# First eight attention units of a fused attention and two-layer network: mask added on TensorE, one exponential per unit, row sums from a column of ones, first loads in program order, weight scaling on ScalarE

## The chip, the cores and the metric

The kernel runs on one core of one Trainium2 chip. The metric is device time in microseconds (us) of one execution; runs of a kernel are given by their median. Engines are called as in the profile: PE is TensorE (PEld its weight loads), DVE is VectorE, ACT is ScalarE, SP is the engine whose queue issues the DMAs here. Every engine runs its own list of instructions strictly in the order of that list, and waits where an operand isn't there yet.

## The reference

Three parts follow each other. The first is attention with 4 batches, 8 heads, 512 local and 32 global positions, 64 numbers a head. A local position sees the global keys and the local keys at most 32 positions away:

```python
s_ll = np.where(np.abs(pos[:, None] - pos[None, :]) <= 32, s_ll, -1e9)
a_l = softmax(np.concatenate([s_lg, s_ll], axis=-1))      # sum + 1e-9 below the line
out_l = np.matmul(a_l, np.concatenate([v_g, v_l], axis=2))
```

Global positions see everything. The result, 2176 rows of 512, goes through `x @ w_in`, a leaky ReLU with a slope of its own for each of the 2048 hidden columns, and `@ w_out`; then through a second layer pair with hard-swish. Weights come to the chip as 64-bit floats seen as integers, so the kernel makes 32-bit floats of them, and each of these is split into a high and a low part for TensorE, so that a product takes three passes (high times high, low times high, high times low).

## The kernel before

**Attention.** A unit is one batch, one half of its 512 rows and one pair of heads: 32 units, taken two at a time. `load` (L166) fetches queries and keys of a unit into `qk_t` (four buffers), `load_v` (L172) its values. `scores` (L182) does the unit's 16 products of 32 rows by 128 keys for two banks of PSUM (one per head). `softmax` (L199) then runs four DVE instructions a unit that add the mask, take the minimum of the negated scores and leave both (L212), four ACT exponentials of 128 columns that also sum their row (L216), and two small DVE instructions that add 1e-9 and invert the sum (L218, L220). `transposes` (L222) does four PE transposes and one ACT copy (L229), `values` (L231) 16 products with the values and one DVE multiplication by the inverted sum (L246), which gives `xo`.

**First layer, block 0.** The tokens of units 0 to 7 (batch 0) are block 0, in two lanes of 256 tokens: lane 0 is units 0 to 3, lane 1 units 4 to 7, four steps (`DELAY`) later. `x_from_attention` (L400) transposes `xo` on PE, and ACT and DVE split it into high and low (L395, L396: `xt`). At each step `h_tile` does 12 products a lane for one hidden chunk (L424), `act` the leaky ReLU on ACT and DVE (L434, L436) and the split of the result (L442, L443: `g`), and `y_tiles` 12 products a lane with the second weights (L455). After block 0 come four more blocks with weights that are on the chip by then, then the second layer pair.

**Weights of the first layer.** There are 32 halves, called raw 0 to raw 31 here, in the order in which they are needed: chunk 0 in, chunk 1 in, chunk 0 out, chunk 2 in, chunk 1 out, chunk 3 in, and so on. Each is a 512 KB DMA into one of five buffers (L94). `to_float32` (L103) makes 32-bit floats of it: a ReLU on ACT over the low words (L109), a scaling of the high words by a power of two on DVE (L113), and two DVE instructions that put the parts together (L117, L119). `split_w` (L123) then casts on ACT to the high part (L125) and subtracts on DVE for the low part (L126). So a half costs ACT two instructions and DVE four:

```python
here(nc.scalar.activation(low, low, AF.Relu, bias=quarter_sb, scale=0.9 * 2.0 ** -29))
if on_dve:
    here(nc.vector.tensor_scalar(out=z, in0=high.bitcast(F32), scalar1=2.0 ** -112, ...))
else:
    here(nc.scalar.activation(z, high.bitcast(F32), AF.Copy, scale=2.0 ** -112))
```

**What sets the order.** The order of each engine's list is made when the kernel is built, by a scheduler with its own estimate of times; `here` (`keep_in_program_order`) ties an instruction to its place in the program. The DMAs of units and weights all go through SP's list, which the scheduler orders too. Buffers of PSUM turn over: what is written next into a bank waits for whoever reads it.

Of the kernel before, what the change touches and what calls it, by code (L numbers as in the profile page):

```python
# [10 lines left out]
F32 = mybir.dt.float32  # L11
# [15 lines left out]
NEG = -1.0e30  # L27
# [15 lines left out]
CONVERT = (3, 4, 5)  # L43
# [12 lines left out]
def fused_kernel(ctx, tc, qkE, vE, qgz, kN, vN, vgN, w1, w2, consts, out):  # L56
# [9 lines left out]

    consts_sb = const.tile([128, 4 * 128 + NJ], F32, name="consts_sb")
# [53 lines left out]
    def split_w(raw, wt, m):  # L123
        z = to_float32(raw)
        nc.scalar.copy(wt[:, m, 0, :], z)  # L125
        nc.vector.tensor_tensor(out=wt[:, m, 1, :], in0=z, in1=wt[:, m, 0, :].bitcast(F32), op=ALU.subtract)  # L126

    class Weights:
# [13 lines left out]
        def fetch(self, upto):  # L142
            while self.got < min(upto, 2 * NJ):
                self.raw[self.got] = load_raw(self.src, *self.seq[self.got])
                self.got += 1

        def convert(self, halves):
            for _ in range(halves):
# [7 lines left out]
                split_w(self.raw.pop(k), self.wt[j], m)  # L156
# [6 lines left out]
    def local_units(att):  # L163
        units = [(b, hf, hp) for b in range(B) for hf in range(2) for hp in range(HP)]
        q_t, k_t, v_t, p_t, rs_t, pt_t, v2 = {}, {}, {}, {}, {}, {}, {}
        def load(u):  # L166
            b, hf, hp = units[u]
            qk = att.tile([128, 256 + UNIT_K], F32, tag="qk", name="qk_t", bufs=PRE + 1)
            nc.sync.dma_start(out=qk, in_=qkE[b, hf, hp])
            q_t[u], k_t[u] = qk[:, 0:256], qk[:, 256:256 + UNIT_K]  # L170

        def load_v(u):  # L172
            b, hf, hp = units[u]
            if u < FIRST_UNITS:
# [24 lines left out]
        def softmax(u, s):  # L199
            b, hf, hp = units[u]  # L200
            if u < FIRST_UNITS:
                if u == 0:
# [4 lines left out]
            st = att.tile([128, 4, 4], F32, tag="st", name="st", bufs=4)
            for i in range(2):
                m = 1 if (hf, i) == (0, 0) else 2 if (hf, i) == (1, 1) else 0
# [9 lines left out]
            rs_t[u] = att.tile([128, 4], F32, tag="rs", name="rs", bufs=FIRST_UNITS)  # L219
# [11 lines left out]
        def values(*us):  # L231
            o = bank("o_ps")
# [44 lines left out]
        load_v(4)  # L277
        load_v(5)
# [663 lines left out]
    W1.fetch(2)  # L942
    k = 0
# [65 lines left out]
def _layout(q_l, k_l, v_l, q_g, k_g, v_g, moe_w_in, moe_w_out, moe_alpha, moe2_w_in, moe2_w_out):  # L1009
# [17 lines left out]
    vE = con(vw.reshape(B, HP, 2, 16, 128, D).transpose(0, 1, 4, 3, 2, 5))  # L1027
# [9 lines left out]
    def chunks(w_in, w_out):  # L1037
# [31 lines left out]
```

## Time and profile before

| | us |
|---|---|
| median of 3 runs | 840.61 (839.18 to 841.01) |
| the profiled execution | 838.92 |
| its span, first to last instruction | 836.8 |
| PE busy in the span | 817.8 (98%) |
| DVE busy | 594.1 (71%) |
| ACT busy | 415.4 (50%) |

The profiled execution is 1.7 us below the median. Outside its span lie 2.1 us. PE is busy nearly always, so the places where it isn't are what there is to look for; "busy" counts pipelined matmuls from start to modelled end, so a slowed row of matmuls can look busy too. A view by stretches gives the busy time of each engine in each; where an engine is busy all the time in a stretch in which PE waits, that engine is the bound there. A group's "idle before" is the time that its engine stood still just ahead of it.

### The profile page before, as it was taken

The numbers are of one execution on the slowest core, as the hardware profiler recorded it, in microseconds if no ns is written. First come the engines' busy times: TensorE is split into PE (matmuls) and PEld (weight loads), VectorE is DVE, ScalarE is ACT, GpSimd is POOL, SyncE is SP. The second block draws the span as 40 slices with busy tenths as digits, with TensorE's granted clock in tenths as the row PEclk, the third lists the DMA queues.
The fourth block names the chain that finished last, engine by engine and source line by source line (L and its number), as shares of the span: only waits on it lengthen the run. The fifth ranks groups of instructions, "written<-read, shape, count | busy, mean of one in ns | idle before, by whom it ended". The sixth has DMA issues, their size and how long they took to land.

```text
span 836.8 us, 18274 instructions
## 1 busy us (share of the span) xinstructions
PE 817.8 (98%) x7228; PEld 740.3 (88%) x7228; DVE 594.1 (71%) x1319; ACT 415.4 (50%) x905; POOL 0.2 (0%) x4
## 2 busy tenths in 40 slices
PE   6889999999999999989999999999999999999997
PEld 4779999888888888878899988889999999999996
DVE  4999995477878786787678847778867678854221
ACT  5876665455656554455454523434543444432222
POOL 0000000000000000000000000000000000000000
PEclk9999999999999999999999999999999999999999
DMA  9976563367768876798575555666675878788872
GB/s 334 340 267 239 181 215 119 109 210 254 272 215 296 270 253 238 256 312 297 182 263 203 166 200 190 193 208 215 201 239 199 295 255 284 243 280 262 276 255 67
DMA packets 72868, 195.70 MB, mean 234 GB/s; under 512 B 7120, under 2 KB 18384, under 8 KB 72784
## 3 DMA queue, kind: packets, MB, share of 16 engines
q1 hardware_dynamic: 72688, 194.42, 68.8%
q8 instruction: 57, 0.93, 0.4%
q14 instruction: 27, 0.22, 0.1%
q10 hardware_dynamic: 96, 0.13, 0.1%
HBM read 152.05 MB, written 42.47 MB: 232 GB/s over the span
## 4 chain that ended last, share of the span: by engine, by line
PE 86%; DVE 6%; DMA 3%; ACT 3%; issue 1%; SPq 0%; DVEq 0%; ACTq 0%
PE y_ps L455 20%; PE h_ps L424 19%; PE o_ps L859 17%; PE k_ps L776 16%; PE h_ps L928 4%; PE o_ps L714 4%; DMA raw<-in_w 2%; PE o_ps L240 1%; PE s_ps L194 1%; DVE z L117 1%; PE pt_ps L227 1%; DVE z L119 1%; DVE wt L126 1%; DVE z L113 1%; PE xt_ps L409 1%
## 5 line engine op out<-in xcount | busy, mean ns | idle before, releaser
L455 PE MATMUL y_ps<-g,wt 128*128 128x256 f32 (+2 forms) x1152 | 209.3, 331 | 3.4 <-ACT g L442 1.7
L424 PE MATMUL h_ps<-xt,wt 128*128 128x256 f32 (+2 forms) x1152 | 206.3, 329 | 1.4 <-DVE xt L396 0.9
L455 PEld LDWEIGHTS y_ps<-g,wt 128*128 128x128 f32 x1152 | 176.5, 189 | 23.0 <-ACT g L442 2.1
L424 PEld LDWEIGHTS h_ps<-xt,wt 128*128 128x128 f32 x1152 | 177.8, 190 | 18.7 <-DVE xt L396 1.1
L859 PE MATMUL o_ps<-ws,gh 128*128 128x256 f32 x784 | 139.4, 283 | 0.0
L776 PE MATMUL k_ps<-bt,ws 128*128 128x512 f32 (+1 forms) x672 | 135.1, 362 | 0.0
L776 PEld LDWEIGHTS k_ps<-bt,ws 128*128 128x128 f32 x672 | 121.2, 188 | 13.0
L859 PEld LDWEIGHTS o_ps<-ws,gh 128*128 128x128 f32 x784 | 120.8, 192 | 0.1
L859 PE MATMUL o_ps<-ws,gl 128*128 128x256 f32 x392 | 107.0, 283 | 0.0
L790 DVE TENSOR_TENSOR gl<-far,gh 128x1024 fp32r<-128x1024 f32 (+1 forms) x56 | 60.9, 1089 | 33.0 <-ACT gh L789 32.7
L789 ACT CAST gh<-far 128x1024 fp32r<-128x1024 f32 (+1 forms) x56 | 52.7, 942 | 62.8 <-PE o_ps L859 58.5
L436 DVE SCALAR_TENSOR_TENSOR t<-t,c_sb,h_ps 128x256 f32<-128x256 f32 (+2 forms) x96 | 55.2, 588 | 32.3 <-ACT t L434 32.0
L859 PEld LDWEIGHTS o_ps<-ws,gl 128*128 128x128 f32 x392 | 73.5, 192 | 0.0
L434 ACT ACTIVATE t<-h_ps 128x512 f32<-128x512 f32 (+2 forms) x84 | 42.8, 511 | 52.9 <-PE h_ps L424 51.2
L442 ACT CAST g<-t 128x512 fp32r<-128x512 f32 (+2 forms) x84 | 45.3, 539 | 43.8 <-DVE t L436 43.7
L443 DVE TENSOR_TENSOR g<-t,g 128x512 fp32r<-128x512 f32 (+2 forms) x84 | 49.2, 587 | 21.3 <-ACT g L442 18.7
L761 ACT ACTIVATE t<-far,half_sb 128x512 f32<-128x512 f32 (+1 forms) x48 | 32.1, 671 | 50.9 <-DVE far L757 49.7
L216 ACT ACTIVATE p<-p,st 128x128 f32<-128x128 f32 x128 | 49.7, 390 | 11.9 <-DVE st L212 11.9
L109 ACT ACTIVATE raw<-raw,quarter_sb 128x512 uint32<-128x512 uint32 x64 | 49.6, 775 | 3.7 <-DMA raw<-in_w 3.7
L117 DVE SCALAR_TENSOR_TENSOR z<-z,raw 128x512 uint32<-128x512 uint32 x64 | 43.7, 691 | 3.3 <-ACT raw L109 0.8
L119 DVE SCALAR_TENSOR_TENSOR z<-raw,z 128x512 uint32<-128x512 uint32 x64 | 43.6, 689 | 0.7
L928 PE MATMUL h_ps<-xt,ws 128*128 128x384 f32 x192 | 36.0, 336 | 0.0
(100 smaller groups left out, 854.8 us busy)
## 6 DMA issues: line engine op xcount, KB each, us to landing
ws<-wo SPq DMA_DIRECT2D x72, 512.0 KB, 4.2
raw<-in_w SPq DMA_DIRECT2D x64, 512.0 KB, 5.4
ws<-wi SPq DMA_DIRECT2D x64, 512.0 KB, 4.6
v_t<-in_vE SPq DMA_DIRECT2D x32, 512.0 KB, 7.1
qk_t<-in_qkE SPq DMA_DIRECT2D x32, 368.0 KB, 5.5
wi<-raw SPq DMA_DIRECT2D x16, 512.0 KB, 3.1
wi<-parts SPq DMA_DIRECT2D x16, 512.0 KB, 4.5
wo<-raw SPq DMA_DIRECT2D x16, 512.0 KB, 4.0
```

Source lines behind the costliest of these rows:

```text
L109: here(nc.scalar.activation(low, low, AF.Relu, bias=quarter_sb, scale=0.9 * 2.0 ** -29))
L117: nc.vector.scalar_tensor_tensor(out=bits, in0=bits, scalar=3, in1=low, op0=ALU.logical_shift_left, op1=ALU.bitwise_or)
L119: nc.vector.scalar_tensor_tensor(out=bits, in0=high, scalar=0x80000000, in1=bits, op0=ALU.bitwise_and, op1=ALU.bitwise_or)
L216: nc.scalar.activation(p[:, n, :], p[:, n, :], AF.Exp, bias=st[:, 1, n:n + 1], scale=-1.0, accum_out=st[:, 2, n:n + 1])
L424: nc.tensor.matmul(ps[:, a:b], lhsT=wts[j][:, 0, wl, 128 * c:128 * c + 128], rhs=xt[c][:, xl, a:b], start=k == 0, stop=k == 3 * NC - 1)
L436: nc.vector.scalar_tensor_tensor(out=t[:, c:d], in0=t[:, c:d], scalar=c1_sb[:, j:j + 1], in1=ps[:, c:d], op0=ALU.mult, op1=ALU.add)
L455: nc.tensor.matmul(y[c][:, a:b], lhsT=wts[j][:, 1, wl, 128 * c:128 * c + 128], rhs=g[:, gl, a:b], start=first, stop=last, skip_group_check ...
L776: nc.tensor.matmul(bank, lhsT=wt[:, wl, at:at + 128], rhs=bt[x][:, c, xl, 0:w], start=first and k == 0, stop=k == 5, skip_group_check=True)
L789: nc.scalar.copy(hi, src)
L790: nc.vector.tensor_tensor(out=lo, in0=src, in1=hi.bitcast(F32), op=ALU.subtract)
L859: mm = nc.tensor.matmul(bank, lhsT=part[:, jp, 128 * c:128 * c + 128], rhs=wo[:, jp, 256 * wl:256 * wl + 256], start=opens, stop=k == NP / ...
L928: nc.tensor.matmul(h, lhsT=wt[:, wl, 128 * c:128 * c + 128], rhs=xt[c][:, xl, 0:w], start=k == 0, stop=k == 3 * NC - 1)
```

## The change

For units 0 to 7 (`FIRST_UNITS` is 8 and was 4; before, those units only had other buffers) the mask is now put into PSUM by a matmul of the identity with the mask, ahead of the score products, which add to it; ACT copies the mask and identity once into a tile of the matmul's type. DVE takes the row maximum of a whole bank (`tensor_reduce`) and subtracts it; one ACT exponential of 512 columns follows for each unit, with no sum. The values of these units get a column of ones (65 columns instead of 64), so the product itself gives the row sum, and DVE adds 1e-9, inverts and multiplies after the product. Units 0 and 1 go through scores one by one. The first loads are tied to program order, with values of units 0 and 1 ahead of queries and keys of units 2 and 3. All 32 halves of first-layer weights (`SCALED_ON_ACT`) have their scaling on ACT.

```diff
-NEG = -1.0e30
+NEG = -2.0 ** 100
-FIRST_UNITS = HP
+FIRST_UNITS = 2 * HP
+ORDERED = 5 * HP // 2
-CONVERT = (3, 4, 5)
+SCALED_ON_ACT = 32
+CONVERT = (2,3,4)
+    mask_r = wp.tile([128, 4 * 128], F32R, tag="w", name="mask_r", bufs=NJ)
...
-    def split_w(raw, wt, m):
-        z = to_float32(raw)
+    def split_w(raw, wt, m, on_dve):
+        z = to_float32(raw, on_dve)
...
-                split_w(self.raw.pop(k), self.wt[j], m)
+                split_w(self.raw.pop(k), self.wt[j], m, k >= SCALED_ON_ACT)
...
+        def first_scores(*us):
+            n, hf = 2 * len(us), units[us[0]][1]
+            s = [bank("s0_ps")[:, 0:128 * n], bank("s1_ps")[:, 0:128 * n]]
+            for h in range(2):
+                mask = mask_r[:, 128 * hf:128 * hf + 256]
+                nc.tensor.matmul(s[h].rearrange("p (e k) -> p e k", k=256), lhsT=mask_r[:, 384:512],
+                                 rhs=mask[:, None, :].to_broadcast([128, len(us), 256]), start=True, stop=False,
+                                 skip_group_check=True)
...
+                            nc.tensor.matmul(s[h][W * g:W * g + W, to:to + 128], lhsT=q[rows, at:at + W],
+                                             rhs=k[rows, o:o + 128], start=False, stop=True, skip_group_check=True)
...
+            for h in range(2):
+                x = s[h].rearrange("p (n k) -> p n k", k=128)
+                nc.vector.tensor_reduce(out=st[:, h, :], in_=x, axis=AX.X, op=ALU.max)
+                nc.vector.tensor_tensor(out=p.rearrange("p e (i h) k -> p h (e i) k", h=2)[:, h], in0=x,
+                                        in1=st[:, h, :, None].to_broadcast([128, n, 128]), op=ALU.subtract)
+            for e, u in enumerate(us):
+                nc.scalar.activation(p[:, e], p[:, e], AF.Exp, scale=0.125)
...
+        def first_values(*us):
...
+                        nc.tensor.matmul(o[W * g:W * g + W, n, :], lhsT=pt[:, n, W * g:W * g + W],
+                                         rhs=v[:, 4 * (n // 2) + g, n % 2, :], start=True, stop=True)
+                nc.vector.tensor_scalar(out=rs[:, 0, :], in0=o[:, :, D], scalar1=1e-9, scalar2=None, op0=ALU.add)
+                nc.vector.reciprocal(out=rs[:, 1, :], in_=rs[:, 0, :])
+                nc.vector.tensor_tensor(out=x.rearrange("p i (h d) -> p (i h) d", h=2), in0=o[:, :, 0:D],
+                                        in1=rs[:, 1, :, None].to_broadcast([128, 4, D]), op=ALU.mult)
...
         load(0)
-        nc.sync.dma_start(out=consts_sb, in_=consts)
+        here(nc.sync.dma_start(out=consts_sb, in_=consts))
+        nc.scalar.copy(mask_r, consts_sb[:, 0:512])
         load(1)
+        load_v(0)
+        load_v(1)
         load(2)
         load(3)
-        load_v(0)
-        load_v(1)
```

The change moves instructions on every engine. The first place is the head of SP's list. `qk_t` is queries and keys of a unit, `v_t` its values, `raw` a half of the weights. Before:

```order
L169 DMA qk_t<-in_qkE 128x736
L255 DMA consts_sb<-in_consts 128x528
L169 DMA qk_t<-in_qkE 128x736 x3
L180 DMA v_t<-in_vE 128x1024 x2
L94 DMA raw<-in_w 128x512
L180 DMA v_t<-in_vE 128x1024 x2
L94 DMA raw<-in_w 128x512
```

And now:

```order
L172 DMA qk_t<-in_qkE 128x736
L309 DMA consts_sb<-in_consts 128x528
L172 DMA qk_t<-in_qkE 128x736
L179 DMA v_t<-in_vR 128x1040 x2
L172 DMA qk_t<-in_qkE 128x736 x2
L99 DMA raw<-in_w 128x512
L179 DMA v_t<-in_vR 128x1040 x2
L99 DMA raw<-in_w 128x512
```

Values of units 0 and 1 stand ahead of queries and keys of units 2 and 3; raw 0 and raw 1 keep their places.

The second place is ACT's list around the softmax of units 4 and 5, with raw 3 to raw 6. L216 and L211 are exponentials, L109 and L111 the ReLU of a raw half, L118 its scaling, L125 and L127 the cast, L434 and L494 the leaky ReLU, L442 and L502 the split of its result, L229 and L281 the copy of transposed probabilities. Before:

```order
L109 ACTIVATE raw<-raw,quarter_sb 128x512
L125 CAST wt<-z 128x512 x2
L216 ACTIVATE p,st<-p,st 128x128 x3
L434 ACTIVATE t<-h_ps 128x256
L216 ACTIVATE p,st<-p,st 128x128 x5
L109 ACTIVATE raw<-raw,quarter_sb 128x512
L434 ACTIVATE t<-h_ps 128x256
L442 CAST g<-t 128x256
L229 COPY pt<-pt_ps 128x512 x2
```

And now:

```order
L111 ACTIVATE raw<-raw,quarter_sb 128x512
L118 ACTIVATE z<-raw 128x512
L494 ACTIVATE t<-h_ps 128x256 x2
L127 CAST wt<-z 128x512
L502 CAST g<-t 128x256 x2
L111 ACTIVATE raw<-raw,quarter_sb 128x512
L211 ACTIVATE p<-p 128x512 x2
L111 ACTIVATE raw<-raw,quarter_sb 128x512
L118 ACTIVATE z<-raw 128x512 x2
L281 COPY pt<-pt_ps 128x512 x2
```

The two exponentials now stand between the ReLU of one raw half and the scaling of it and of the next.

The third place is the same piece on DVE: L207 is the row maximum, L208 the subtraction, L119 and L121 the two instructions that put a raw half together, L128 its low part, L496 and L503 the leaky ReLU and the split. Now:

```order
L119 SCALAR_TENSOR_TENSOR z<-z,raw 128x512
L207 TENSOR_REDUCE st<-s_ps 128x4 x2
L121 SCALAR_TENSOR_TENSOR z<-raw,z 128x512
L496 SCALAR_TENSOR_TENSOR t<-t,c_sb,h_ps 128x256 x2
L128 TENSOR_TENSOR wt<-z,wt 128x512
L208 TENSOR_TENSOR p<-s_ps,st 128x4x128
L503 TENSOR_TENSOR g<-t,g 128x256
L208 TENSOR_TENSOR p<-s_ps,st 128x4x128
L503 TENSOR_TENSOR g<-t,g 128x256
L119 SCALAR_TENSOR_TENSOR z<-z,raw 128x512 x2
L121 SCALAR_TENSOR_TENSOR z<-raw,z 128x512 x2
```

The next raw halves (the two L119 near the end) follow right behind the subtractions and the split; the scaling of the high words is gone from the list.

## Rows read from the trace of the kernel before

**Rows 1.** Stretches: busy us of PE, PEld, DVE, ACT, POOL; clock, DMA share, GB/s.

```profile
0.00:20.86 20.86, 14.29 (x287) 9.84 (x287) 9.43 (x56) 11.92 (x42) 0.20 (x4) 0.92 0.91 334
20.86:49.36 28.50, 25.00 (x432) 19.90 (x432) 27.10 (x103) 24.23 (x80) 0.00 (x0) 0.94 0.89 321
49.36:62.50 13.14, 11.84 (x92) 11.24 (x93) 12.54 (x28) 9.33 (x18) 0.00 (x0) 1.00 0.75 266
62.50:134.50 72.00, 71.72 (x907) 68.72 (x906) 66.92 (x177) 46.76 (x111) 0.00 (x0) 1.00 0.61 210
...
10.00:15.00 5.00, 4.55 (x78) 3.07 (x77) 2.28 (x20) 5.00 (x24) 0.00 (x0) 0.88 1.01 392
...
21.00:25.00 4.00, 4.00 (x63) 2.75 (x63) 4.00 (x9) 2.60 (x5) 0.00 (x0) 0.57 1.03 408
```

**Rows 2.** PE in order of time: start, us, instructions [idle before, releaser].

```profile
20.86 0.36 PE L424 MATMUL h_ps<-xt,wt 128*128 128x256 f32 x1
...
49.36 3.13 PE L424 MATMUL h_ps<-xt,wt 128*128 128x256 f32 x24 [0.91 <-DVE xt L396]
53.68 0.75 PE L455 MATMUL y_ps<-g,wt 128*128 128x256 f32 x4 [1.19 <-ACT wt L125]
...
59.28 3.39 PE L455 MATMUL y_ps<-g,wt 128*128 128x256 f32 x24
```

**Rows 3.** All engines around the scores of units 1 to 3, in order of time.

```profile
6.82 0.67 PE L194 MATMUL s_ps<-qk_t 64*32 64x128 f32 x32 [1.61 <-DMA qk_t<-in_qkE]
...
8.70 0.66 PEld L194 LDWEIGHTS s_ps<-qk_t 64*32 64x32 f32 x32 [0.27 <-DMA qk_t<-in_qkE]
```

**Rows 4.** DVE from raw 1 on, in order of time.

```profile
17.98 0.43 DVE L113 TENSOR_SCALAR z<-raw 128x512 f32<-128x512 f32 x1 [0.76 <-DMA raw<-in_w]
18.32 0.68 DVE L119 SCALAR_TENSOR_TENSOR z<-raw,z 128x512 uint32<-128x512 uint32 x1
18.92 0.68 DVE L117 SCALAR_TENSOR_TENSOR z<-z,raw 128x512 uint32<-128x512 uint32 x1
19.53 0.75 DVE L396 TENSOR_TENSOR xt<-xt_ps,xt 128x256 fp32r<-128x256 f32 x2
20.19 0.75 DVE L246 TENSOR_TENSOR xo<-o_ps,rs 128x256 f32<-128x256 f32 x2
```

**Rows 5.** Groups of DVE by shape, whole trace: xcount, busy us, mean ns, idle before.

```profile
L443 DVE TENSOR_TENSOR g<-t,g 128x512 fp32r<-128x512 f32 x44 | 30.4, 690 | 15.4 <-ACT g L442 13.4 <-PE o_ps L240 1.4
...
L113 DVE TENSOR_SCALAR z<-raw 128x512 f32<-128x512 f32 x64 | 26.9, 421 | 0.8 <-DMA raw<-in_w 0.8
...
L343 DVE TENSOR_REDUCE gst<-gs_ps 128x1 f32<-128x512 f32 x8 | 5.5, 689 | 1.3 <-PE gs_ps L332 1.0
...
L396 DVE TENSOR_TENSOR xt<-xt_ps,xt 128x512 fp32r<-128x512 f32 x8 | 5.1, 685 | 1.8 <-ACT xt L395 1.7
```

**Rows 6.** Groups of ACT by shape, whole trace.

```profile
L216 ACT ACTIVATE p<-p,st 128x128 f32<-128x128 f32 x128 | 49.7, 390 | 11.9 <-DVE st L212 11.9
L109 ACT ACTIVATE raw<-raw,quarter_sb 128x512 uint32<-128x512 uint32 x64 | 49.6, 775 | 3.7 <-DMA raw<-in_w 3.7
...
L125 ACT CAST wt<-z 128x512 fp32r<-128x512 f32 x32 | 19.4, 616 | 12.6 <-DVE z L119 12.4
...
L347 ACT ACTIVATE gp<-gs_ps,gst 128x512 f32<-128x512 f32 x8 | 5.5, 683 | 7.5 <-DVE gst L346 4.7 <-PE y_ps L455 2.8
```

**Rows 7.** ACT in order of time: two copies in a row, and one ReLU.

```profile
15.68 1.05 ACT L229 COPY pt<-pt_ps 128x512 f32<-128x512 f32 x2
17.98 0.79 ACT L109 ACTIVATE raw<-raw,quarter_sb 128x512 uint32<-128x512 uint32 x1 [1.25 <-DMA raw<-in_w]
18.66 0.62 ACT L395 CAST xt<-xt_ps 128x256 fp32r<-128x256 f32 x2
```

**Rows 8.** DVE's busy time on L113 alone, in one of the stretches.

```profile
20.86:49.36 28.50, 3.19 (x8) 0.94 0.89 321
```

**Rows 9.** The chain that ended last: two mask instructions of DVE side by side.

```profile
37.52 0.20 DVE p L212
37.73 0.20 DVE p L212
```

More of the change, by code (lines that the diff above doesn't have):

```diff
@@ L87, in fused_kernel, with load_raw @@
                          stop=True)
-    def load_raw(src, j, m):
+    here = tc.keep_in_program_order
+    def load_raw(src, j, m, place=lambda x: x):
         raw = work.tile([128, 512], I64, tag="raw", name="raw", bufs=RAW)
-        nc.sync.dma_start(out=raw, in_=src[j, :, 512 * m:512 * m + 512])
+        place(nc.sync.dma_start(out=raw, in_=src[j, :, 512 * m:512 * m + 512]))
         return raw
-    here = tc.keep_in_program_order
     def to_float32(raw, on_dve=True):
@@ L143, in fetch @@
             while self.got < min(upto, 2 * NJ):
-                self.raw[self.got] = load_raw(self.src, *self.seq[self.got])
+                self.raw[self.got] = load_raw(self.src, *self.seq[self.got], here if self.got < RAW else lambda x: x)
                 self.got += 1
@@ L254, in local_units @@
         load(0)
-        nc.sync.dma_start(out=consts_sb, in_=consts)
+        here(nc.sync.dma_start(out=consts_sb, in_=consts))
+        nc.scalar.copy(mask_r, consts_sb[:, 0:512])
+        here(nc.vector.tensor_scalar(out=c1_sb, in0=alpha_sb, scalar1=-1.0, scalar2=1.0, op0=ALU.mult, op1=ALU.add))
         load(1)
+        load_v(0)
+        load_v(1)
         load(2)
         load(3)
-        load_v(0)
-        load_v(1)
         yield
@@ L265, in local_units @@
         pairs = [(u, u + 1) for u in range(0, n, 2)]
-        scores(*pairs[0])
+        for u in pairs[0]:
+            scores(u)
+        load(4)
+        load(5)
         yield
         scores(*pairs[1])
-        here(nc.vector.tensor_scalar(out=c1_sb, in0=alpha_sb, scalar1=-1.0, scalar2=1.0, op0=ALU.mult, op1=ALU.add))
-        load(4)
-        load(5)
+        load_v(4)
+        load_v(5)
         yield
@@ L1026, in _layout @@
     vw = np.stack([v_ext[:, :, W * start_of(a):W * start_of(a) + 128] for a in range(16)], axis=2)
-    vE = con(vw.reshape(B, HP, 2, 16, 128, D).transpose(0, 1, 4, 3, 2, 5))
+    vE = con(vw.reshape(B, HP, 2, 16, 128, D).transpose(0, 1, 4, 3, 2, 5)[1:])
+    v0 = con(vw.reshape(B, HP, 2, 16, 128, D).transpose(0, 1, 4, 3, 2, 5)[0])
+    v0 = np.concatenate([v0, np.ones((HP, 128, 16, 2, 1), np.float32)], axis=4)
+    vR = con(np.stack([v0[:, :, 8 * hf:8 * hf + 8] for hf in range(2)]))
     qg = pair(q_g).transpose(1, 2, 4, 0, 3).reshape(HP, 2, D, B * SG)
```

71 lines of the change are left out of this document (50 added, 21 removed).

## The prediction

> **What bounds the kernel now.** I first read the busy time by stretches. From 62.50 us on PE is busy 71.72 of 72.00 us [rows 1], so what the change does later than that can only cost. Ahead of it PE has holes. Up to the first product of the first layer at 20.86 us [rows 2] PE is busy 14.29 of 20.86 us, and part of that is warm-up; from there to 49.36 us, where both lanes start to run together (24 products of chunk 4), it is busy 25.00 of 28.50 us, and from there to 62.50 us 11.84 of 13.14 us [rows 1]. What counts is how early PE reaches the state of 62.50 us, and with how much of its work done; the rest of the kernel follows shifted, since PE is full from there on.
>
> Next, who is full where PE waits. In 20.86 to 49.36 us DVE is busy 27.10 of 28.50 us and ACT 24.23 [rows 1]. Both are close to full, DVE is the bound, and PE's waits name it: 0.91 us for `xt` ahead of the 24 products, and then 1.19 us for ACT's cast of a weight [rows 2]. Ahead of 20.86 us the bound is transfers: 392 GB/s at a DMA share of 1.01 [rows 1]; the scores of unit 1 wait 1.61 us for queries and keys, those of unit 3 start at 8.70 us when theirs land [rows 3], and DVE waits 0.76 us for raw 1, which lands at 17.98 us [rows 4].
>
> **The prices.** A DVE instruction of 512 columns lasts 0.68 us, but the next begins 0.60 us after it (18.32, 18.92, 19.53) and two of 256 columns take 0.66 us (19.53 to 20.19) [rows 4]: I count 0.60 and 0.33. The row maximum and the subtraction have rows of the same size from PSUM, 0.689 and 0.685 us [rows 5], so 0.60 each too. The mask instruction of before follows itself after 0.21 us [rows 9]. On ACT two copies of 512 columns take 1.05 us, so 0.54 each in a row, and the ReLU of a half is followed after 0.68 us [rows 7]. The exponential of 512 columns lies between a cast (0.616 us) and the exponential that also sums (0.683 us) [rows 6]; I take the cast's end, since nothing is summed: 0.54 in a row. The scaling on ACT reads every second word like the ReLU (0.775 us) and writes without gaps like the cast (0.616 us) [rows 6]; I take 0.66 us, 0.58 in a row, as the write and the missing bias make it more like the cast. It replaces 0.421 us on DVE [rows 5].
>
> The Trainium skill ("ScalarE: Activation LUTs", section What ACT_TABLE_LOAD costs) states 186 ns + 0.833 ns a column for an ACTIVATE with immediate scale, which gives 0.61 us as an estimate; by it the ten scalings counted below would cost 0.5 us less. The cast's row agrees with it (0.616 us), the strided ReLU does not (0.775 us) [rows 6].
>
> **Parts that cost nothing.** The mask matmuls: 4 of 256 and 6 of 512 columns are 16 times 256 columns, at 0.13 us for one (24 in 3.13 us [rows 2]) 2.1 us, of which half stand ahead of the first layer while PE waits for transfers, and half in 20.86 to 49.36 us, where PE has 3.5 us to spare [rows 1]. If that cover were gone: +1.0 us. The column of ones is 1 in 64 of the value products, under 0.1 us. The mask's copy on ACT delays the first scores by 0.6 us, but unit 1's keys come later (6.82 us [rows 3]) anyway. ACT is relieved by the exponentials: 32 of 0.39 us [rows 6] are 12.5 us, and 8 of 0.54 us are 4.3 us; it gets 32 scalings of 0.58 us, 18.6 us.
>
> **The start: +2.4 us.** The new order of loads puts values of units 0 and 1, 1.06 MB, ahead of the keys of units 2 and 3. At 392 GB/s [rows 1] that is 2.7 us, so unit 3's keys land at 8.7 + 2.7 = 11.4 us. Behind them: scores 0.7 us; DVE four instructions of 0.60 us and three short ones of 0.19 us (15.1 us); two exponentials (16.2 us). ACT's list then has the cast of raw 0, which waits until DVE has put raw 0 together (17.7 us), two copies of transposed probabilities, and only then the ReLU and the scaling of raw 1: 17.7 + 3 x 0.54 + 0.68 + 0.58 = 20.6 us. DVE's first instruction on raw 1 was at 18.92 us [rows 4] and is now at 20.7 us. Unit 2's `xo`, which opens lane 0, was at 20.19 us [rows 4]. Now two instructions of 0.60 us, two of 0.19 and one of 0.33 us stand between: 20.7 + 1.9 = 22.6 us, 2.4 us late. If the keys land as before, the wait for raw 1 at 17.98 us is what is late next, and the lag is some 1.2 us: ReLU, scaling (1.26 us) now run one after the other, where DVE's scaling ran beside the ReLU. If the two values delay them by 4 us it is 3.6 us.
>
> **Lane 0 alone, 20.86 to 49.36 us before: +1.8 us.** DVE loses the eight scalings, 3.19 us [rows 8]. For the softmax of units 4 to 7 it loses 16 mask instructions of 0.21 us (3.4 us) and gets 4 maxima and 4 subtractions of 0.60 us (4.8 us): +1.4 us. The new list has two more halves finished, 4 instructions of 0.60 us, ahead of the products of chunk 4: +2.4 us, which is done early and comes off again. So DVE has 27.1 - 3.2 + 1.4 + 2.4 = 27.7 us of work. The gain of the move is small; its price is waits. ReLU, scaling, DVE's two instructions, cast and DVE's subtraction now form one chain that crosses from ACT to DVE and back, and ACT's list, which was free to run ReLUs ahead, is tied to DVE in the middle. Walking down the new lists with the prices above, DVE waits: 0.8 us for the cast of raw 2; 0.6 us for the scaling of raw 3 (cast, split, ReLU and scaling stand in a row on ACT, 2.1 us, against 1.5 us on DVE); 2.2 us for that of raw 4, where two exponentials wait for DVE's second subtraction (33.9 us), and behind them a ReLU and the scaling (0.54 + 0.54 + 0.68 + 0.58 = 2.3 us), while DVE has one split left to do; 0.9 us for raw 8; and four of 0.2 to 0.4 us, 1.0 us. Together 5.5 us, against 1.4 us before (28.50 less 27.10). So the stretch lasts 27.7 + 5.5 = 33.2 us instead of 28.5; less 2.4 us of work done early, less 0.5 us for four matmuls that PE has done more by then, +1.8 us.
>
> **Both lanes, 49.36 to 62.50 us before: +1.7 us.** The new ACT list has the ReLU of raw 11 behind the split of chunk 4, which waits for the leaky ReLU on DVE, which waits for PE. From the end of chunk 4 to the low part of raw 11 stand leaky ReLU, split, ReLU, scaling on ACT (2.3 us), DVE's parts, and two copies, a ReLU, a split and another ReLU ahead of the cast on ACT (3.0 us): 8.5 us, in which PE has 6.5 us to do (24 products of chunk 5, 8 transposes, 24 of the second weights). PE waits 2.0 us, and 1.0 us for raw 12. Before, PE waited 13.14 - 11.84 = 1.3 us here [rows 1]. So +1.7 us.
>
> **The sum.** 2.4 + 1.8 + 1.7 = +5.9 us: the profiled execution's 838.92 would be 844.8 us. The median is 1.7 us above that execution, so the forecast for the median is 840.61 + 5.9 = 846.5 us. Bounds of the prices: cheap scaling and maximum (ACT at 0.5 us, DVE at 0.4 us) and early keys take 3.4 us off, dear ones (0.68 us in a row) and late keys add 2.1 us: 843.1 to 848.6 us.
>
> **Rivals.** *DVE's relief decides.* If the waits for ACT don't arise, because ACT runs ahead at each of the places above, DVE's 27.10 of 28.50 us [rows 1] is the bound that falls: -3.2 + 1.4 us in the second stretch, and in the third the four scalings there (4 x 0.33 = 1.3 us of 12.54 us busy) cover PE's 1.3 us of waits. With the start as before that is -3.1 us: 837.5 us. It decides if the scaling of raw 4 is ready before DVE has done the subtractions of units 4 and 5. For it: ACT has 4.27 us to spare in the second stretch. Against it: the exponentials stand between, in the order shown. The Trainium skill ("Perfetto Trace Analysis", section Identifying the Most-Contended Engine) says to find the engine with the highest occupancy and improve that first; by that rule, with DVE at 95% and ACT at 85%, the move should gain. The trace agrees on who is fuller; that occupancy decides here is what I doubt.
>
> *The ends meet.* Keys land early (lag 1.2 us), the later waits on ACT come to half: +1.2 + 1.8 - 2.0 + 0.5, +1.5 us or less: 841 to 842 us, near no change.
>
> *The clock falls too.* After PE's waits the granted clock was 0.57 in 21 to 25 us, part of the time at 1.2 instead of 2.4 GHz [rows 1]. Longer waits can bring that into a stretch where PE is the one waited for: 4 us at 0.57 lose 1.7 us, twice that 3.4 us on top of the sum: 850 us.
>
> **How the numbers follow.** Forecast 846.5 us (844 to 849) with a chance of 0.57; relief of DVE, 837.5 us (835 to 840), 0.23; the ends meet 0.13; clock on top 0.07. A measurement of this kernel tells apart about 0.2%, 1.7 us. Faster by more: 0.23 (nearly all of the relief, and a little of the ends). Within: 0.12. Slower by more: 0.65. For the range I leave out the lower half of the relief and the top of the clock: 837.5 to 850 us.
>
> **What would show it.** Right: the first product of the first layer near 23 us, the 24 products of chunk 4 near 57 us, DVE idle several us before 57 us, its releaser ACT; PE idle before the products of chunk 6 for a raw half. Wrong: first product before 21.5 us (the loads did no harm), or chunk 4 before 49 us with DVE full (relief). If PE is busy all the time from 60 us and the span is still longer, the cause lies in later blocks, which I count as shifted only.

## The result, and the profile after

The changed kernel takes 845.51 us (median of 5 runs, 843.95 to 846.54) against 840.61 (839.18 to 841.54): a ratio of 1.0065, with an interval of 1.0052 to 1.0079. It is slower by 0.65%, 4.9 us; the forecast was 846.5. The two profiled spans differ by 7.5 us (844.3 against 836.8), mostly because the profiled execution of before lies 1.7 us under its median and that of after 0.6 us above. One kernel below, `no_act_scaling`, has times but no usable trace, since its profiled execution was disturbed (granted clock 0.751).

The head of the page after:

```profile
span 844.3 us, 18189 instructions
...
PE 823.1 (97%) x7238; PEld 744.4 (88%) x7238; DVE 587.8 (70%) x1243; ACT 426.6 (51%) x882; POOL 0.2 (0%) x4
```

DVE is busy 6.3 us less than the 594.1 us of before, ACT 11.2 us more, and the kernel is slower. The stretches of after, cut where those of before are cut in [rows 1] (first product of the first layer, 24 products of chunk 4, products of chunk 6) and at the first product of block 1. The columns are as there: length, then busy us of PE, PEld, DVE, ACT, POOL.

```profile
0.00:22.19 22.19, 17.40 (x292) 11.96 (x293) 11.03 (x33) 10.97 (x18) 0.20 (x4) 0.87 0.92 342
22.19:54.95 32.76, 26.91 (x440) 21.83 (x439) 28.00 (x77) 25.30 (x62) 0.00 (x0) 0.92 0.81 295
54.95:68.21 13.26, 11.72 (x91) 11.52 (x89) 8.22 (x19) 8.87 (x17) 0.00 (x0) 0.91 0.55 171
68.21:157.70 89.49, 88.13 (x1153) 84.37 (x1153) 70.69 (x191) 67.50 (x162) 0.00 (x0) 1.00 0.57 191
```

The stretch of lane 0 is 4.3 us longer (32.76 against 28.50), although DVE's busy time in it hardly rose (28.00 against 27.10): DVE now stands still for 4.8 us instead of 1.4. Where it stands still, in order of time (last column: idle before, and releaser):

```profile
19.59 0.69 DVE L119 SCALAR_TENSOR_TENSOR z<-z,raw 128x512 uint32<-128x512 uint32 x1 [1.50 <-ACT z L118]
...
21.32 0.41 DVE L233 TENSOR_TENSOR xo<-o_ps,rs 128x256 f32<-128x256 f32 x1
...
25.57 0.69 DVE L128 TENSOR_TENSOR wt<-z,wt 128x512 fp32r<-128x512 f32 x1 [0.69 <-ACT wt L127]
...
27.42 0.70 DVE L119 SCALAR_TENSOR_TENSOR z<-z,raw 128x512 uint32<-128x512 uint32 x1 [0.82 <-ACT z L118]
...
35.55 1.29 DVE L119 SCALAR_TENSOR_TENSOR z<-z,raw 128x512 uint32<-128x512 uint32 x2 [2.09 <-ACT z L118]
...
48.81 0.69 DVE L119 SCALAR_TENSOR_TENSOR z<-z,raw 128x512 uint32<-128x512 uint32 x1 [0.84 <-ACT z L118]
```

Ahead of the first product, 19.59 and 21.32 stand against 18.92 and 20.19 in [rows 4]. L118 is the scaling on ACT, L119 DVE's first instruction on the scaled half, L127 the cast, L128 the subtraction for the low part, L233 the `xo` of a unit (21.32 is unit 2). ACT's own list ahead of the longest of these waits (L211 is the exponential, L208 DVE's subtraction):

```profile
33.16 1.15 ACT L211 ACTIVATE p<-p 128x512 f32<-128x512 f32 x2 [1.02 <-DVE p L208]
34.21 0.76 ACT L111 ACTIVATE raw<-raw,quarter_sb 128x512 uint32<-128x512 uint32 x1
34.87 1.21 ACT L118 ACTIVATE z<-raw 128x512 f32<-128x512 f32 x2
```

ACT waits 1.02 us for DVE, does two exponentials and a ReLU, and only then the scaling for which DVE has been waiting since 33.46: the two lists wait for each other in turn. PE meets a later wait of this kind, for raw 11, at the products of chunk 6; the longest wait of PE between chunk 4 and chunk 6 was 1.19 us before [rows 2].

```profile
68.21 0.39 PE L484 MATMUL h_ps<-xt,wt 128*128 128x256 f32 x1 [1.54 <-ACT wt L127]
68.93 1.34 PE L484 MATMUL h_ps<-xt,wt 128*128 128x256 f32 x9 [0.34 <-DVE wt L128]
```

### The profile page after: what moved, and what is told of

The parts are those of the page before. It is cut to its first block, busy times and chain, and to the rows that moved or that the text cites. A ratio compares the mean times of both kernels' runs of the same rounds, so it can differ in the third digit from the quotient of the medians.

```text
span 844.3 us, 18189 instructions
## 1 busy us (share of the span) xinstructions
PE 823.1 (97%) x7238; PEld 744.4 (88%) x7238; DVE 587.8 (70%) x1243; ACT 426.6 (51%) x882; POOL 0.2 (0%) x4
## 4 chain that ended last, share of the span: by engine, by line
PE 85%; ACT 5%; DVE 5%; DMA 2%; issue 1%; SPq 0%; ACTq 0%; DVEq 0%
PE y_ps L515 19%; PE h_ps L484 19%; PE o_ps L919 16%; PE k_ps L836 16%; PE h_ps L988 4%; PE o_ps L774 4%; ACT raw L111 1%; PE o_ps L294 1%; PE s_ps L251 1%; DVE z L119 1%; ACT p L268 1%; PE pt_ps L279 1%; PE xt_ps L469 1%; DVE z L121 1%; DMA qk_t<-in_qkE 1%
## 5 line engine op out<-in xcount | busy, mean ns | idle before, releaser
L484 PE MATMUL h_ps<-xt,wt 128*128 128x256 f32 (+2 forms) x1152 | 208.0, 331 | 2.3 <-ACT wt L127 1.5
L484 PEld LDWEIGHTS h_ps<-xt,wt 128*128 128x128 f32 x1152 | 179.4, 192 | 19.3 <-ACT wt L127 1.7
L496 DVE SCALAR_TENSOR_TENSOR t<-t,c_sb,h_ps 128x256 f32<-128x256 f32 (+2 forms) x96 | 55.2, 587 | 35.0 <-ACT t L494 34.9
L494 ACT ACTIVATE t<-h_ps 128x512 f32<-128x512 f32 (+2 forms) x84 | 43.0, 513 | 52.6 <-PE h_ps L484 51.5
L502 ACT CAST g<-t 128x512 fp32r<-128x512 f32 (+2 forms) x84 | 45.2, 539 | 38.7 <-DVE t L496 38.6
L503 DVE TENSOR_TENSOR g<-t,g 128x512 fp32r<-128x512 f32 (+2 forms) x84 | 49.2, 586 | 22.2 <-ACT g L502 19.7
L119 DVE SCALAR_TENSOR_TENSOR z<-z,raw 128x512 uint32<-128x512 uint32 x64 | 44.0, 690 | 11.9 <-ACT z L118 8.7
L111 ACT ACTIVATE raw<-raw,quarter_sb 128x512 uint32<-128x512 uint32 x64 | 49.6, 775 | 1.0 <-DMA raw<-in_w 0.8
L121 DVE SCALAR_TENSOR_TENSOR z<-raw,z 128x512 uint32<-128x512 uint32 x64 | 43.8, 688 | 0.8
L268 ACT ACTIVATE p<-p,st 128x128 f32<-128x128 f32 x96 | 37.3, 390 | 6.8 <-DVE st L264 6.8
```

The source lines that it names most:

```text
L119: nc.vector.scalar_tensor_tensor(out=bits, in0=bits, scalar=3, in1=low, op0=ALU.logical_shift_left, op1=ALU.bitwise_or)
L121: nc.vector.scalar_tensor_tensor(out=bits, in0=high, scalar=0x80000000, in1=bits, op0=ALU.bitwise_and, op1=ALU.bitwise_or)
L484: nc.tensor.matmul(ps[:, a:b], lhsT=wts[j][:, 0, wl, 128 * c:128 * c + 128], rhs=xt[c][:, xl, a:b], start=k == 0, stop=k == 3 * NC - 1)
L496: nc.vector.scalar_tensor_tensor(out=t[:, c:d], in0=t[:, c:d], scalar=c1_sb[:, j:j + 1], in1=ps[:, c:d], op0=ALU.mult, op1=ALU.add)
L503: nc.vector.tensor_tensor(out=g[:, 1, a:b], in0=t[:, a:b], in1=g[:, 0, a:b].bitcast(F32), op=ALU.subtract)
```

## Experiments

Three parts can be taken apart: the new softmax with the mask on PE, the fixed order of first loads (with `CONVERT`, the steps at which raw halves are converted), and the scaling on ACT. The ratio is to the kernel before, run beside each, with medians of 839.48 to 840.61 us. "h to c6" is the time from the first product of the first layer to the products of chunk 6, and the last two columns are DVE in it, added up from the views by stretches. These columns come from one profiled execution of each; that of `keys_first_dve_scaling` took 845.30 us, 2.2 more than its median, the others at most 1.7 from theirs. In `five_on_act` less of PE's work lies ahead of chunk 6 than in the others (see there).

| kernel | median us | ratio [95%] | first product at | h to c6 | DVE busy | DVE idle |
|---|---|---|---|---|---|---|
| before | 840.61 | 1 | 20.86 | 41.65 | 39.6 | 2.0 |
| changed | 845.51 | 1.0065 [1.0052, 1.0079] | 22.19 | 46.02 | 36.2 | 9.8 |
| no_act_scaling | 843.85 | 1.0042 [1.0029, 1.0054] | | | | |
| act_scaling_alone | 842.62 | 1.0028 [1.0015, 1.0040] | 20.41 | 45.05 | 37.3 | 7.7 |
| loads_alone | 843.72 | 1.0038 [1.0025, 1.0052] | 23.65 | 43.15 | 39.4 | 3.7 |
| softmax_alone | 846.06 | 1.0069 [1.0053, 1.0084] | 22.75 | 46.06 | 40.1 | 5.9 |
| keys_first_dve_scaling | 843.08 | 1.0048 [1.0025, 1.0071] | 20.13 | 48.05 | 40.7 | 7.4 |
| softmax_per_unit | 842.61 | 1.0040 [1.0026, 1.0055] | 19.50 | 45.91 | 41.8 | 4.1 |
| keys_first | 844.41 | 1.0059 [1.0040, 1.0078] | 19.22 | 47.30 | 38.4 | 8.9 |
| four_back_on_dve | 842.52 | 1.0033 [1.0022, 1.0044] | 21.65 | 44.29 | 38.0 | 6.3 |
| both_mended | 841.76 | 1.0028 [1.0017, 1.0039] | 20.08 | 44.71 | 39.6 | 5.1 |
| scaling_on_pool | 845.15 | 1.0065 [1.0049, 1.0080] | 21.38 | 44.35 | 37.8 | 6.6 |
| five_on_act | 839.68 | 1.0003 [0.9993, 1.0013] | 21.06 | 39.13 | 35.9 | 3.2 |
| lists_reordered | 838.28 | 0.9980 [0.9970, 0.9991] | 19.54 | 40.61 | 39.5 | 1.1 |

**Each part undone or alone.** First the scaling, taken out of the changed kernel:

```diff
-SCALED_ON_ACT = 32
+SCALED_ON_ACT = 0
```

> The changed kernel with all 32 scalings back on DVE (new softmax and fixed order of loads kept). Theory 1 (scaling on ACT ties the lists of ACT and DVE together, and the waits of DVE for ACT are most of the loss): the start keeps its lag, a little less than 1.3 us; DVE has 3.2 us more work in the stretch of lane 0, but the waits for the scalings of raw 3, 4 and 8 (0.8, 2.1, 0.8 us) and PE's waits for raw 11 (1.9 us) go. Time 841.5 to 843.5 us against 840.6 of the kernel before and 845.5 of the changed one. Theory 2 (new softmax and late keys cost, the relief of DVE gains): without the relief of 3 us it is slower than the changed kernel, 847 to 849 us. Theory 3 (only the start counts): as the changed kernel, 844.5 to 846 us.

Measured 843.85 us. It is near theory 1 (841.5 to 843.5) and rules out theory 2 (847 to 849): without the "relief" the kernel is not slower but a little faster than the changed one, with intervals that just touch. But the scaling is then worth 1.7 of 4.9 us, not most of it. Second, the scaling alone, in the kernel before, for the 32 halves of the first layer:

```diff
-        z = to_float32(raw)
+        z = to_float32(raw, False)
```

> The kernel before with nothing changed but the scaling, which is on ACT for all 32 halves of the first layer. Theory 1: the start loses some 0.6 us (ReLU and scaling in a row), DVE loses 3.2 us of work in the stretch of lane 0 and gets more than that in waits for ACT; here the 32 short exponentials of units 4 to 7 are still on ACT as well. Time 842 to 845 us. Theory 2: DVE's relief of 3 us counts, 837 to 839 us. Theory 3: about as before, 840 to 841.5 us.

842.62 us, as theory 1 said. The stretches of lane 0 and of both lanes:

```profile
20.41:52.95 32.54, 26.91 (x433) 21.91 (x432) 26.65 (x101) 29.68 (x90) 0.00 (x0) 0.90 0.82 302
52.95:65.46 12.51, 11.54 (x92) 11.14 (x93) 10.68 (x20) 10.06 (x18) 0.00 (x0) 1.00 0.73 249
```

Here ACT is the full engine (29.68 of 32.54 us) and DVE waits 5.9 us in the first of the two. The move took 2.3 us off DVE from the first product to chunk 6 and gave it 5.7 us of waits. Third, the order of loads alone. The cut shows the swap; the run also ties the first loads to program order, gives eight units buffers of their own, fetches raw 2 earlier and has `CONVERT = (2, 3, 4)`:

```diff
         load(1)
-        load(2)
-        load(3)
         load_v(0)
         load_v(1)
+        load(2)
+        load(3)
```

> The kernel before with the fixed order of first loads (values of units 0 and 1 ahead of keys of units 2 and 3, raw 2 earlier, eight units with buffers of their own), but with the old softmax and with the scaling on DVE. Theories 1 and 3: the keys of unit 3 land at 11.3 us instead of 8.7, and the first product of the first layer is late by up to 2.4 us; since the four mask instructions of a unit are 0.84 us together, some 1 to 2 us in the end: 841 to 843 us. Theory 2: the same start, 842 to 843 us. If the order of loads is harmless because raw 1 at 18 us decides: 840 to 841 us.

843.72 us, slower than any theory had it, with the first product 2.8 us late. Fourth, the new softmax alone, which in the changed kernel is

```diff
-ORDERED = 5 * HP // 2
-SCALED_ON_ACT = 32
-CONVERT = (2,3,4)
+ORDERED = 0
+SCALED_ON_ACT = 0
+CONVERT = (3, 4, 5)
```

with the sequence of first loads of before.

> The kernel before with the new softmax of eight units alone; the loads are free for the scheduler again, which puts raw 0 and raw 1 ahead of the values of units 0 and 1 here, and the scaling is on DVE. Theory A: the new softmax costs nothing by itself, ACT loses 8 us of work and DVE gets 1.4 us: 839.5 to 841.5 us, unless the late values hold up the first products. Theory B: 842 to 843.5 us.

846.06 us, against both theories; with the loads free, the scheduler put raw 0 and raw 1 ahead of the values, and the first product came 1.9 us late. So this run mixes two things. The cleaner one keeps the fixed order and its `CONVERT`, with `load(2)` and `load(3)` ahead of `load_v(0)` and `load_v(1)`, and has the scaling on DVE:

```diff
-SCALED_ON_ACT = 32
+SCALED_ON_ACT = 0
```

> Only the new softmax of eight units is left of the change: the order of loads is fixed but with keys of units 2 and 3 ahead of the values, and all 32 scalings are on DVE. Theory A (late keys and the scaling on ACT carry the loss, the new softmax costs nothing): 840 to 842 us. Theory B (the new softmax costs DVE 1.4 us in the stretch of lane 0, and that stretch is bound by DVE): 842 to 844 us, about the 843.85 of the kernel with late keys.

843.08 us: theory A falls. Neither of the two parts that I had blamed is left, the first product even comes 0.7 us early, and the loss is 0.48%. The fixed order apart from the keys is still in this kernel, so the 0.48% is not shown to be the softmax alone.

```profile
20.13:55.81 35.68, 28.60 (x449) 24.00 (x447) 32.31 (x89) 22.17 (x55) 0.00 (x0) 0.93 0.82 296
55.81:68.18 12.37, 11.21 (x82) 10.76 (x81) 8.38 (x17) 7.72 (x15) 0.00 (x0) 0.89 0.48 162
```

DVE is busy 1.1 us longer than before from the first product to chunk 6 and idle 5.4 us longer. One of its waits is 2.02 us, where a maximum over the bank of two units needs the score products of both; PE waits 3.4 us for an exponential that needs both subtractions. Whether handling two units at once is the reason:

```diff
-            for h in range(2):
-                x = s[h].rearrange("p (n k) -> p n k", k=128)
+            for e, u in enumerate(us):
+                for h in range(2):
+                    x = s[h].rearrange("p (n k) -> p n k", k=128)[:, 2 * e:2 * e + 2]
```

> The kernel with the new softmax alone, keys first and scaling on DVE (843.08 us), with maximum and subtraction done for one unit after the other: eight DVE instructions of 256 columns for a pair of units instead of four of 512, so that the exponential of the first unit of a pair doesn't wait for the subtraction of the second. DVE gets 0.24 us more work a pair. Theory A (handling two units at once makes the exponentials late, PE waits 3.4 us in one place for one of them): that wait becomes 1 to 2 us, 841 to 842.3 us. Theory B (the place of the subtractions in DVE's list, behind the work on raw halves, makes them late): 842.7 to 844 us.

842.61 us, between the two ranges. DVE's idle time fell from 7.4 to 4.1 us and the wait of 2.02 us for the scores to 0.45, but DVE's work rose by 1.1 us, and the ratios (1.0040 and 1.0048) have intervals that overlap. The earlier kernel's profiled execution lay 2.2 us above its median, so the drop in idle time is not shown to come from the edit alone. What in the new softmax costs, DVE's added work or its place in the list, stays open.

**The two mends.** The keys first, in the changed kernel, and nothing else (the scaling stays on ACT):

```diff
             load(1)
-            load_v(0)
-            load_v(1)
             load(2)
             load(3)
+            load_v(0)
+            load_v(1)
```

> The changed kernel with queries and keys of units 2 and 3 loaded ahead of the values of units 0 and 1, as in the kernel before; the order is still fixed, everything else stays. The loads alone cost 3.5 us (843.72 against 840.2), with the first product of the first layer 2.8 us late. Theory A (in the changed kernel, too, late keys are a large part of the loss): unit 3's keys land near 8.7 us again, the first product of the first layer comes 0.5 to 1.3 us earlier than 22.19 us, and the time is 842.5 to 844 us against 845.5. Theory B (the lag of the start is swallowed by the waits between ACT and DVE that come after it): the first product comes earlier, the products of chunk 6 don't, and the time stays at 844.8 to 846 us.

844.41 us, between the two theories; the interval overlaps that of the changed kernel. The first product comes 3.0 us earlier than there, and by chunk 6 only 1.7 us of that are left:

```profile
19.22:54.71 35.49, 30.67 (x450) 25.24 (x448) 29.86 (x80) 25.83 (x61) 0.00 (x0) 0.86 0.82 304
54.71:66.52 11.81, 10.03 (x82) 9.59 (x81) 8.55 (x18) 9.34 (x19) 0.00 (x0) 1.00 0.58 183
```

The granted clock is 0.86 over the whole stretch of lane 0, which two rows of PE show directly: after a wait of 2.57 us, 12 products with the second weights take 2.93 us and the next 12 with the first 2.91 us, while these 12 took 1.68 us in the changed kernel (L484 at 34.78 us). The granted clock around the first of them is 0.50, the lower of the two levels (1.2 of 2.4 GHz), and 1.00 around the row of the changed kernel (second view).

```profile
29.57 2.93 PE L565 MATMUL y_ps<-g,wt 128*128 128x256 f32 x12 [2.57 <-ACT g L552]
...
35.00 2.91 PE L534 MATMUL h_ps<-xt,wt 128*128 128x256 f32 x12
...
29.50:32.50 3.00, 2.92 (x12) 2.64 (x12) 2.98 (x6) 1.72 (x4) 0.00 (x0) 0.50 0.56 168
```

```profile
34.78 1.68 PE L484 MATMUL h_ps<-xt,wt 128*128 128x256 f32 x12
...
34.70:36.50 1.80, 1.80 (x16) 1.67 (x14) 0.95 (x2) 1.80 (x5) 0.00 (x0) 1.00 0.68 277
```

And the four scalings that the waits name, back on DVE:

```diff
-                split_w(..., k >= SCALED_ON_ACT)
+                split_w(..., k in (3, 4, 8, 11))
```

> The changed kernel with the scaling of raw 3, 4, 8 and 11 back on DVE, the four for which DVE waits 0.82, 2.09 and 0.84 us and PE 1.9 us in the changed kernel; the other 28 stay on ACT. Theory A (these waits are the price of the scaling on ACT): they go, DVE gets 4 times 0.42 us, so 842.5 to 844 us against 845.5. Theory B (the list of ACT is the bound, and another scaling or split takes their place, as it was with the scaling on POOL): 845 to 846 us.

842.52 us, theory A. Four of 32 scalings give back 3.0 us, and all 32 no more (843.85): the price of the move hangs on these four, where DVE and PE waited. DVE is busier by 1.8 us and idle 3.5 us less:

```profile
21.65:54.77 33.12, 26.86 (x448) 22.56 (x447) 29.48 (x81) 23.53 (x58) 0.00 (x0) 0.95 0.84 303
54.77:65.94 11.17, 10.06 (x84) 9.62 (x81) 8.54 (x18) 8.37 (x18) 0.00 (x0) 1.00 0.53 168
```

Both edits together:

> The changed kernel with both mends: keys of units 2 and 3 ahead of the values of units 0 and 1, and the scaling of raw 3, 4, 8 and 11 back on DVE. If the two are independent: 842.5 us of the four on DVE less the 1 us that the keys brought, 841 to 842 us. If the start is swallowed by later waits, as it was with the keys alone (first product 1.6 us earlier than in the kernel before, chunk 2's products still 5 us later): 842 to 843 us.

841.76 us, in the range for two independent mends (841 to 842), but the interval overlaps that of the four alone: putting the keys first adds little that can be measured.

**A third engine.** The 32 scalings on POOL:

```diff
-            here(nc.scalar.activation(z, high.bitcast(F32), AF.Copy, scale=2.0 ** -112))
+            here(nc.gpsimd.tensor_scalar(out=z, in0=high.bitcast(F32), scalar1=2.0 ** -112, ...))
```

> The changed kernel with the 32 scalings on POOL, which is idle in the kernel (0.2 us busy). ACT's list then has no scaling that stands behind exponentials and splits. Theory 1: the waits at raw 3, raw 4 and raw 8 (3.7 us) fall away or become small, if one scaling on POOL lasts under some 2 us; DVE keeps its relief: 840 to 842.5 us, that is 3 to 5 us below the changed kernel. Theory 2 (new softmax and late keys cost): no difference to the changed kernel, 845 us. What one scaling lasts on POOL no row shows so far; if it is over 3 us, POOL becomes the bound of the raw halves and the kernel is slower than 846 us by either theory.

845.15 us, no different from the changed kernel; theory 2's number, but not by its reason. The first row is POOL's group in this kernel, the next two are DVE's first instruction on a half and its split of `g`; the last two are the same groups of DVE in the changed kernel (columns: count, busy us, mean ns, idle before).

```profile
L121 POOL TENSOR_SCALAR z<-raw 128x512 f32<-128x512 f32 x32 | 56.0, 1757 | 73.0 <-DVE wt L132 53.4 <-DMA raw<-in_w 19.4
...
L123 DVE SCALAR_TENSOR_TENSOR z<-z,raw 128x512 uint32<-128x512 uint32 x32 | 24.5, 764 | 7.0 <-POOL z L121 4.3 <-issue 1.5 <-ACT raw L114 0.6
...
L554 DVE TENSOR_TENSOR g<-t,g 128x512 fp32r<-128x512 f32 x12 | 10.6, 880 | 1.2 <-ACT g L553 1.2
```

```profile
L119 DVE SCALAR_TENSOR_TENSOR z<-z,raw 128x512 uint32<-128x512 uint32 x32 | 21.9, 690 | 9.4 <-ACT z L118 8.7 <-DMA raw<-in_w 0.5
...
L503 DVE TENSOR_TENSOR g<-t,g 128x512 fp32r<-128x512 f32 x12 | 8.3, 688 | 1.4 <-ACT g L502 1.3
```

A scaling takes 1.76 us there (0.42 on DVE, 0.68 on ACT), POOL waits 53.4 us for DVE to give back one of the two buffers of `z`, and some of DVE's own instructions get longer. The tie between the lists is not gone; it has another name.

**Is it only the order?** A control, the kernel before with one number of the change (here, as in `five_on_act` and `act_scaling_alone`, the first units' values also come from an input array of their own, in transfers of the same size):

```diff
-CONVERT = (3, 4, 5)
+CONVERT = (2, 3, 4)
```

> A control: the kernel before with one number of the change alone, the three steps at which a raw half is converted ahead of block 0, (2, 3, 4) instead of (3, 4, 5). No instruction is added or taken away; the scheduler puts the first 60 us of the lists of PE, DVE, ACT and SP together in another order. Theory A (what costs in each part of the change is its own work or its later loads): 840 to 841.2 us, no difference to before. Theory B (the lists of before are a tight fit, DVE waits 1.4 us in 28.5, and any other order costs waits, which is a good part of what each of the parts alone cost, 2.4 to 5.9 us): 842 us or more.

838.28 us, a ratio of 0.9980: theory B falls, since this other order of 60 us of lists costs nothing. It even beats both kernels, below either range. DVE is idle for 0.1 us in the stretch of lane 0, and the first product comes 1.3 us early; the granted clock there is 1.00 against 0.94 before, and no run separates what the lists and what the clock gain:

```profile
0.00:19.54 19.54, 14.11 (x287) 9.76 (x287) 8.57 (x54) 12.18 (x43) 0.20 (x4) 0.91 0.91 337
19.54:47.68 28.14, 24.00 (x432) 18.99 (x431) 28.04 (x105) 24.39 (x80) 0.00 (x0) 1.00 0.98 357
47.68:60.15 12.47, 11.79 (x95) 11.20 (x93) 11.46 (x27) 9.03 (x17) 0.00 (x0) 1.00 0.68 235
```

Last, the move where ACT has room, in the kernel before:

```diff
-                split_w(self.raw.pop(k), self.wt[j], m)
+                split_w(self.raw.pop(k), self.wt[j], m, k not in (2, 9, 10, 11, 12))
```

> The kernel before with the scaling of five halves only on ACT: raw 2 and raw 9 to 12, where ACT stood idle in the kernel before (0.7 to 1.9 us at a time at 25 us and from 50 to 58 us) and DVE was full. Theory A (DVE's relief is worth something where ACT has room): DVE loses 0.4 us by raw 2 and 1.7 us around 50 to 60 us, where PE waited 1.3 us: 838.5 to 840.3 us, faster than both kernels. Theory B (any other order of the lists costs waits): 841 to 843 us.

839.68 us, ratio 1.0003: in theory A's range only because the kernel before ran at 839.48 us beside it; there is no gain. In the table chunk 6 begins 2.3 us earlier than before, but that is one product, put ahead of 20 products with the second weights (first view); before, 24 of those came first [rows 2] and all 24 products of chunk 6 followed (second view):

```profile
60.19 0.33 PE L534 MATMUL h_ps<-xt,wt 128*128 128x256 f32 x1
60.36 2.64 PE L565 MATMUL y_ps<-g,wt 128*128 128x256 f32 x20
62.84 2.92 PE L534 MATMUL h_ps<-xt,wt 128*128 128x256 f32 x23
```

```profile
62.51 3.04 PE L424 MATMUL h_ps<-xt,wt 128*128 128x256 f32 x24
```

So with the same work done PE is not early. DVE's busy time up to that product fell by 3.7 us (five scalings are 2.1; the rest is work that now stands behind), and by block 1 the kernel is 1.0 us late, after a wait of PE of 1.19 us for a cast. DVE's relief did not reach PE here.

## Why the prediction was right, step by step

The sign and the size hold, and so does the mechanism of the scaling as far as DVE goes: its relief turns into waits for ACT, and with four of the 32 scalings back on DVE 3.0 of the 4.9 us are gone. But the terms erred in both directions and partly offset each other, so that the sum came out near is in part luck: 5.9 us lies between the 7.5 of the profiled spans and the 4.9 of the medians. And a part of the loss that no run separates comes with the new softmax, which I had booked as DVE work only.

| term | predicted us | measured us |
|---|---|---|
| start (first product) | +2.4 | +1.33 (22.19 less 20.86) |
| stretch of lane 0 | +4.7 (33.2 less 28.5) | +4.26 (32.76 less 28.50) |
| both lanes, with work done early taken off | -1.2 (1.7 less 2.9) | +0.1 (13.26 less 13.15) |
| chunk 6 to block 1 | 0 | +1.2 (89.49 less 88.32) |
| from there to the end | 0 | +0.6 |
| sum | +5.9 | +7.5 |

*Start.* DVE's first instruction on raw 1 was at 19.59, not 20.7: raw 0 was put together on DVE a microsecond earlier than I had walked it. I said that with keys on time the lag would still be 1.2 us; `keys_first` has the first product 1.6 us earlier than the kernel before, so late keys cost the first product of the changed kernel 3.0 us. Where the 1.6 us come from stays open. The new softmax takes away DVE's waits for the sums of ACT's exponentials (the longest is 1.64 us; first view, before), but `lists_reordered` has the old softmax and the same wait, and its first product is 1.3 us early all the same: there DVE does unit 2's `xo` at 18.87 us, ahead of raw 1, instead of 20.19 (second view). `keys_first` has the same `CONVERT`.

```profile
15.18 0.17 DVE L218 TENSOR_SCALAR st<-st 128x4 f32<-128x4 f32 x1 [1.64 <-ACT p L216]
```

```profile
15.11 0.17 DVE L285 TENSOR_SCALAR st<-st 128x4 f32<-128x4 f32 x1 [1.64 <-ACT p L283]
...
18.87 0.75 DVE L315 TENSOR_TENSOR xo<-o_ps,rs 128x256 f32<-128x256 f32 x2
```

*The mask matmuls* stood among the parts that cost nothing, at 2.1 us and covered. They are busy 4.6 us, more than twice that; what they cost no run tried.

```profile
L190 PE MATMUL s_ps<-mask_r 128*128 128x512 f32 (+1 forms) x10 | 4.6, 538 | 0.5 <-ACT mask_r L310 0.5
```

*Lane 0.* The waits came where I put them: 0.69 us for the cast of raw 2 (0.8 predicted), 0.82 for raw 3 (0.6), 2.09 for raw 4 (2.2), 0.84 for raw 8 (0.9); only the "others" are 0.3 instead of 1.0. DVE's work is 28.00 (27.7). The scaling lasts 0.68 us on ACT (0.66 taken). The Trainium skill ("ScalarE: Activation LUTs", What ACT_TABLE_LOAD costs) gave 0.61 as an estimate; the trace differs. The strided ReLU, which the prediction set against that figure, also has a bias operand, so it is no test of it. `four_back_on_dve` takes raw 3, 4, 8 and 11 off ACT and gives back 3.0 us, so what the scaling costs hangs on these four; how it reaches PE is less clear (the clock, below).

*Both lanes.* PE waits 1.88 us for raw 11 (1.54 ahead of chunk 6's first product and 0.34 behind it; 2.0 predicted) and not at all for raw 12 (1.0). But the step that took 2.4 us off for work that DVE has done early failed: DVE is busy 8.22 us here instead of 12.54, and the stretch is no shorter, since PE has its 11.7 us to do and the chain from leaky ReLU to raw 11 sets its end. Work done early on DVE was worth nothing here, where DVE is not the bound. *Later* I counted a shift only; besides those 0.34 us PE waits another 0.9 us for a cast at 114.6 us.

*What the sum attributes.* I had booked the new softmax as 1.4 us of DVE work. With the keys first and the scaling on DVE 0.48% of loss is left, but that kernel has the rest of the fixed order of loads too, and no run has that order with keys first and the old softmax. So how much of it is the softmax stays open. The order of loads with late keys costs 0.38% alone and the scaling 0.28%. The three sum to 1.14% and the whole is 0.65%; part of the excess is that the fixed order is in two of them. What undoing a part gives back (0.23% for the scaling, 0.06% for the keys, within its interval) is not what it costs alone.

*The rivals.* Relief of DVE (837.5): DVE's busy time from first product to chunk 6 did fall, by 3.4 us, but its idle time rose by 7.8. The Trainium skill ("Perfetto Trace Analysis", Identifying the Most-Contended Engine) would work on the fullest engine first; for the move of all 32 scalings the runs show the contrary (1.0028 alone), for five of them nothing (1.0003). The clock on top (850): partly there, 0.92 and 0.91 in the two stretches against 0.94 and 1.00 in [rows 1]; the sum had no term for it, and no run isolates its price. It may be large. Ahead of chunk 6 PE is idle 12.2 us instead of 11.4, but busy 56.0 instead of 51.1, with the mask matmuls in it. In `four_back_on_dve` PE is busy 3.9 us less than in the changed kernel and idle 1.6 us more, at a granted clock of 0.95 and 1.00 in the two stretches. "Busy" counts slowed rows, so the time that PE lost shows as slower rows more than as waits; whether the clock fell because of the waits or would have fallen anyway stays open.

## What to carry to other kernels

Moving work from a full engine to a less full one did not pay here: DVE lost work and then waited for ACT. Look at what stands ahead of the moved work in the receiver's list. Four of the 32 moved scalings carried what the move cost; the five moved to places where the receiver had room cost nothing, and gained nothing either. An operand that crosses between two in-order lists twice ties both. A point such as "the first product of chunk 6" compares two kernels only if the same work lies ahead of it in both. And do the control: one number of this change, taken alone, made the kernel 0.2% faster, which the 0.65% that the whole lost had hidden.

## What the runs showed of the hardware

With the scaling on POOL, some of DVE's instructions of 512 columns with both inputs in SBUF took longer: in the mean 880 ns instead of 688 for the split of `g` and 764 instead of 690 for the first instruction on a half, one of them 1.13 us, but 691 instead of 686 for the second instruction on a half, while DVE's instruction that reads PSUM stayed at 474 ns (475 in the changed kernel). The Trainium skill ("SBUF — State Buffer", SBUF: two separate sides) says that a DVE instruction with two SBUF inputs and a POOL instruction that reads SBUF lock each other out of a port that they share; the traces agree in the first two groups, and the third shows that not every such instruction is held up. A scaling that takes 0.42 us on DVE took 1.76 us on POOL in the mean of 32 (1.51 to 2.09).
